# An FNet and SwiGLU mix on one core: x loaded in one piece, a weight's load ahead of two stores, the comparisons of O1 placed anew, and a register load ahead of the last stores

## The chip, the core and the metric

The kernel runs on one core of a Trainium2 chip. The metric is the device time of one execution in microseconds (us), from the program's launch to its end on that core; lower is better. A profile of one execution comes with it. Its span runs from the first to the last instruction, and its times count from the span's start. The engines have short names: PE is TensorE (matrix products), PEld its weight loads, DVE is VectorE, ACT is ScalarE, POOL is GpSimd, and SP is SyncE, which does nothing here but issue transfers (DMAs) and decide the branch at the end.

## The reference

```
x = A_x                                      # 2048 x 512
g = sigmoid((x * gate_w).sum(-1))            # one gate per row
a = dft_hid_re and dft_hid_im applied to x   # along the 512 columns
y = dft_seq_re @ a_re - dft_seq_im @ a_im    # along the 2048 rows
b = (silu(x @ w1) * (x @ w3)) @ w2           # 512 -> 1376 -> 512
out = g * y + (1 - g) * b
```

All in float32. The four DFT matrices are inputs like the others; the kernel may use their structure only if they have it.

## The kernel before

**Numbers in two parts.** TensorE multiplies a shortened float32 format (F32R). Each operand is split into a high part, which ScalarE writes as a copy (`high`, L113), and a low part, the rest, which VectorE makes by a subtraction (`low`, L116). One product of two operands is then three matmuls: high by high, high by low, low by high (`mm3`).

**The SwiGLU branch** comes first, until about 210 us. The products with w1 and w3 run as 22 items, each a chunk of 128 of the 1376 columns by half of the rows; the first is written out by itself, the others are `gate_up(1)` to `gate_up(21)`. A two-by-two block scheme needs seven block products instead of eight for an item; for it VectorE makes sums and differences of x's blocks (tiles `xs_B`, then `xo`) and of w's blocks (`ws`, then the high and low parts `wa` and, from the sums `wu` of `sums_wb`, `wb`). `gate_up(n)` writes out one item by hand: the order of its products, copies and stores is the order of the lines, on every engine. Its `prod(x, n, 4, 4)` is copied by ScalarE into h (L361), the next item's first product waits for a copy out of its PSUM bank, and ScalarE's silu L398 empties the last product. h goes to DRAM by two POOL stores (`store_h`, L320) and its tile has two buffers, so a new h waits until the stores of the one before last have landed. `low_wb` (L244) also stores wb to DRAM by POOL (L248), because the second half of the rows uses it again. The load of a later chunk's w (`load_w`, L198) is POOL's as well; `NEXT_W` says which item issues which load, and at (n, 1) it comes behind `low_wb`.

**The head.** SyncE loads the first quarter of w's first chunk, then x's block B11 in two halves (`load_xo(0, "B11", 2)`, tiles of 256 KB each), then the rest of that w and the other blocks of x. While these come, PE runs eleven warm-up products (L413). The first half of B11 is split by ScalarE and VectorE together and the first products `C` start with it; the next step, `a`, needs the rest of w.

**The stage of w2** (products H, about 210 to 324 us) multiplies h, loaded back, by w2. Beside it the other engines do two things: they prepare forms of x for the Fourier branch, and they compare the given DFT matrices with themselves. A DFT matrix is full of equal and opposite rows. So only one representative piece (`rep`) of each group O1a, O1b, O2 and E2 is multiplied, and for every other piece VectorE subtracts it from, or adds it to, the representative (`differ`, L730 to L736), and ScalarE sums the absolute values (`add_up`, L741).

**The planner.** These comparisons are tasks in a list. The code is run once when the program is built, and every call `work(engine, us)` puts as many ready tasks of that engine at that place in its order as fit the budget `us`. A task costs 1.2 (VectorE) or 1.1 (ScalarE), may pass the budget by 0.3, and is only taken when its load was asked for at least `LAG` calls before (4 in the stage of w2 and in O1). `work_until` issues all that is left.

**The Fourier branch** (from 324 us). For each of two parts p the products of O1 run into PSUM; ScalarE copies one bank to `e` (L1234); VectorE makes its sum and difference with the other bank (L1235, L1236); `high` and `low` make z_O1 of it. Then follow O2 and E2. Ten output units (L1282 on) multiply z by the hidden DFT; VectorE adds each product times the gate to the SwiGLU part, (1 - g) * b (L1303), and SyncE stores the rows (L1305). Units 0 to 5 have two parts of 128 rows, units 6 to 9 one.

**The end.** When all absolute sums are there, `verdict` (L568, L570) reduces them on VectorE behind unit 3. `sum_flags` (L573) adds them over the partitions on PE, ahead of unit 7's products, and `see_flags` (L576) compares the result behind unit 7's sums. Behind the last unit all five engines load that flag into a register (L1318) and branch (L1325): if the matrices aren't DFT matrices, a second, plain computation follows. In the profiled execution the branch is skipped. SyncE then waits for the last stores to land, and the program ends.

Of the kernel before, what the change touches and what calls it, by code (L numbers as in the profile page):

```python
# [9 lines left out]
I32 = mybir.dt.int32  # L10
# [5 lines left out]
D = 512  # L16
# [14 lines left out]
def fnet_swiglu_gate_kernel(  # L31
# [25 lines left out]
    nc = tc.nc  # L57
# [54 lines left out]
    def high(hi, src):  # L112
        nc.scalar.activation(hi, src, AF.Copy)  # L113

    def low(hi, lo, src):
        nc.vector.tensor_sub(lo, src, hi.bitcast(F32))  # L116
# [36 lines left out]
    XO, ST = {}, {}  # L153
    XRAW = ("B12", "B11", "B21", "B22")
# [9 lines left out]
            XO[2] = xo1.tile([P, 2, 2, 512], F32R, tag="xo6", name="xo1_6")  # L164
        return XO[2]

    def load_xo(g, k, pieces=1):

        if g not in XO:
            XO[g] = (xo1 if g else xo0).tile([P, 2, 7 - g, 2, 512], F32R, tag="xo", name=f"xo{g}")  # L170
        ST[g, k] = wide(f"xs{g}_{k}")
        n = 1024 // pieces
        for i in range(pieces):
            nc.sync.dma_start(ST[g, k][:, i * n : i * n + n], xt[g, XRAW.index(k), :, i * n : i * n + n])

    OPS = ("B11", "B21", "B22", "T1", "T2", "T3", "T4")
    SUMS = {"T1": ("B12", "B11"), "T2": ("B22", "T1"), "T3": ("B22", "B12"), "T4": ("B21", "T2")}
# [14 lines left out]
    def back(w):  # L192
        return w >= NC and SETS[w] > 0

    def load_w(w, lo=0, hi=4, by=nc.gpsimd):
        if lo == 0:
            WS[w] = f4_a.tile([P, 4, 256], F32, tag=f"f4_{4 + w % (LOOK + 1)}", name=f"ws{w}")
        by.dma_start(WS[w][:, lo:hi].rearrange("p a n -> p (a n)"), w13[SETS[w], :, lo * 256 : hi * 256])  # L198
# [27 lines left out]
    def sums_wb(w):  # L226

        r = WS.pop(w)
        u = WU[w] = wup.tile([P, 4, 256], F32, tag="wu", name=f"wu{w}")
        nc.vector.tensor_add(u[:, 2], r[:, 3], r[:, 2])  # L230
        nc.vector.tensor_sub(u[:, 0], u[:, 2], r[:, 0])
        nc.vector.tensor_sub(u[:, 1], r[:, 0], r[:, 3])
        nc.vector.tensor_sub(u[:, 3], r[:, 1], u[:, 0])
# [5 lines left out]
    def high_wb(w):  # L239
        for half in range(2):  # L240
            new_wb(w, half)
            high(*wb_parts(w, half)[::2])
# [89 lines left out]
    NEXT_W = {}  # L332
    for w in range(LOOK + 3, len(SETS)):
        v = w - LOOK - 1
        at = (WSET.index(v) - LOOK, 0) if back(v) else (WSET.index(v) - 1, 1)
        NEXT_W.setdefault(at, []).append(w)

    def gate_up(n):
        last = NI - 1
        x, s1 = G.pop(n)  # L340
        z = bank(6 + n % 2, f"Z{n}")
        if n >= NI - 3:
            h = HR[n - NI + 3] = wide(f"h{n}")
        else:
            h = hp.tile([P, 1024], F32, tag="h", name=f"h{n}")
        u2, g1 = h[:, :512], h[:, 512:]
        u4 = u4p.tile([P, 512], F32, tag="u4", name=f"u4_{n}")
        nw = WSET[n + 1] if n < last else 0
        if nw == 0 or nw == WSET[n] or len(WB.get(nw, ())) == 2:
            nw = None  # L350
        elif back(nw):
            load_wb(nw, 1)
            nw = None
        wa = WSET[n + LOOK + 1] if n + LOOK < last else 0
        if wa in WA or wa == 0:
            wa = None
        for w in NEXT_W.get((n, 0), ()):
            load_w(w, 0, 3)

        prod(x, n, 4, 4, False, True)  # L360
        nc.scalar.activation(u2, x, AF.Copy)  # L361
        run(early, n)
        prod(z, n, 5, 5, True, True)
        run(ahead, n)
        nc.scalar.activation(u4, z, AF.Copy)
        run(second, n)
        if nw is not None and n > 1:
            sums_wb(nw)
        if n + LOOK <= last:
            first1(n + LOOK)  # L370
        if nw is not None and n > 1:
            high_wb(nw)
        if n + 2 < NI - 3 and back(WSET[n + 2]):
            load_wb(WSET[n + 2], 0)
        prod(x, n, 3, 3, False, True)
        nc.vector.tensor_add(u4, u4, x)  # L376
        if nw is not None and n == 1:
            sums_wb(nw)
            high_wb(nw)
        if nw is not None:  # L380
            low_wb(nw)
        for w in NEXT_W.get((n, 1), ()):
            load_w(w, 0, 3 if back(w) else 4)
        run(mid, n)
        prod(z, n, 2, 6, False, True)
        nc.vector.tensor_add(u2, u2, z)
        nc.vector.tensor_mul(u2, s1, u2)  # L387
        store_h(n, 0, u2)
        if wa is not None:
            new_wa(wa)  # L390
            parts_a = wa_parts(wa, 0, 3)
            high(parts_a[0], parts_a[2])
        if n + LOOK <= last:
            first2(n + LOOK)
        if wa is not None:
            low(*parts_a)
        prod(x, n, 6, 2, False, True)
        nc.scalar.activation(g1, x, AF.Silu)  # L398
        put_score(n, 1, x)
        if n + LOOK <= last:  # L400
            gate1(n + LOOK)
        nc.vector.tensor_mul(g1, g1, u4)
        store_h(n, 1, g1)
        run(at_end, n)
# [1 line left out]

    ctx.enter_context(tc.manual_schedule())
    load_w(0, 0, 1, nc.sync)
    load_xo(0, "B11", 2)
    warm = nc.const_aps.tensor(1.0, [P, 512], mybir.dt.bfloat16)  # L410
    wps = bank(7, "wps")
    for n in range(WARM):
# [143 lines left out]
    n = NI - 1 - LOOK  # L556
# [5 lines left out]
    flag = tail[:, 144:160]  # L562
# [545 lines left out]
    for m, (half, c) in enumerate(HSTEPS):  # L1108
        i = m % NC
# [11 lines left out]
        h, w = HT[m][1], WT[i]  # L1121
# [91 lines left out]
    def load_nb(u):  # L1213
        n, k = UNITS[u][3], FIRST[u]
        if k < 8:
            NB[u] = NBK[k // 2]
            return
        NB[u] = wide(f"nbr{u}")
        nc.sync.dma_start(NB[u].rearrange("p (k n) -> p k n", k=2)[:, :n],
                          nbsp[k - 8 : k - 8 + n].rearrange("k p n -> p k n"))  # L1220
# [4 lines left out]
    for p in range(2):  # L1225
        t = next_two(f"O1_{p}")
        ps = t[:, :512], t[:, 512:]
        for par in range(2):
            forms(ps[par][:, :256], ps[par][:, 256:], ("O1a", "O1b"), (par,), p)
            if par == 0:  # L1230
                work("A", 1.2 if p else 2.4)
                work("D", 1.3)
        e, s = wide(f"e{p}"), wide(f"s{p}")
        nc.scalar.activation(e[:, :512], ps[0], AF.Copy)  # L1234
        nc.vector.tensor_add(s[:, :512], e[:, :512], ps[1])  # L1235
        nc.vector.tensor_sub(s[:, 512:], e[:, :512], ps[1])  # L1236
        free(e)
        t = parts(f"z_O1{p}").rearrange("p h a n -> p h (a n)")
        high(t[:, 0], s)
        low(t[:, 0], t[:, 1], s)  # L1240
        free(s)
        Z["O1", p] = t
        work("D", 1.2)
    t = parts("z_O2").rearrange("p h a n -> p h (a n)")
    two = next_two("O2")
    for p in range(2):
# [18 lines left out]

    for u in range(6, len(UNITS)):
        load_nb(u)
    z_E = yp.tile([P, 2, 2, 516], F32R, tag="z_E2", name="z_E2")

    def even(p):  # L1270
# [8 lines left out]
    for u, (kind, za, zb, n, swap) in enumerate(UNITS):  # L1279
        if u == 4:  # L1280
            even(1)
        ps = next_two(f"Y{u}")  # L1282
        if u == 7:
            sum_flags(ps)

        def zs(p, at):
            return [Z[kind, p][:, h, at : at + P] for h in range(2)]

        evens = ps[:, 250:510].rearrange("p (b n a) -> p b n a", b=2, a=2)
        odds = ps[:, 512:768].rearrange("p (b n a) -> p b n a", b=2, a=2)  # L1290
        chain_two(evens, [(zs(0, za), same_d(0, 130)), (zs(1, zb), both_d(0, 130))])
        chain_two(odds, [(zs(1, za), same_d(130, 258)), (zs(0, zb), both_d(130, 258))])
        r = yp.tile([P, 1024], F32, tag=f"r{u % 6}", name=f"r{u}")
        nb = NB.pop(u)

        def pair(lo, hi):
            return ps[:, lo : lo + 2 * (hi - lo)].rearrange("p (a m) -> p a m", a=2)[:, :, :P]

        for i in range(n):
            k = FIRST[u] + i  # L1300
            rv, nv = (v[:, i * D : i * D + D].rearrange("p (a h n) -> p a h n", a=2, h=2) for v in (r, nb))
            for h, src in enumerate((pair(380, 640), pair(251, 512)) if i ^ swap else (pair(250, 512), pair(381, 640))):
                nc.vector.scalar_tensor_tensor(rv[:, :, h], src, g_pos[:, k : k + 1], nv[:, :, h],  # L1303
                                               op0=ALU.mult, op1=ALU.add)
        nc.sync.dma_start(out[FIRST[u] : FIRST[u] + n].rearrange("k p n -> p k n"),  # L1305
                          r.rearrange("p (k n) -> p k n", k=2)[:, :n])
        if FIRST[u] > 7:
            free(nb)
        if u < 2:
            work("A", 3.6)  # L1310
            work("D", 1.3)
        if u == 2:
            work_until(set(range(n_late)))
        if u == 3:
            verdict()
        if u == 7:
            see_flags(ps)
    bad = nc.values_load(flag.bitcast(I32)[0:1, 2:3], min_val=0, max_val=0x3F800000,  # L1318
                         skip_runtime_bounds_check_because="a comparison's result, 0.0 or 1.0")
    close(zo_a_cm, lp_cm)  # L1320
    close(mov_cm, sp_cm, hh_cm, f4d_cm, y_cm)

# [242 lines left out]
```

## Time and profile before

| | us |
|---|---|
| median of 3 runs | 362.36 (361.52 to 362.67) |
| the profiled execution | 362.3 |
| its span | 360.5 |
| PE busy in the span | 350.8 (97%) |
| DVE busy | 310.0 (86%) |
| ACT busy | 234.2 (65%) |
| POOL busy | 102.8 (29%) |

The profile is read by its views. The waits say which engine stood idle for whom: total, number of times, longest. A row of the timeline has the start, the length, the engine, the line, the operation, the tiles (out<-in), their shapes and the number of instructions merged in it, and in brackets the idle time just before with what ended it. The starts of neighbouring instructions lie closer than their lengths, since one begins while the one before still writes. The DMA rows have the number of transfers, KB each and the median from issue to landing. A row for a stretch has its length, the busy time of an engine with the number of instructions, the granted clock of TensorE, the DMA engines' share and GB/s.

### The profile page before, as it was taken

How to read it: one execution, taken by the hardware profiler on the slowest of the kernel's cores; microseconds unless marked ns; L12 is line 12 of the kernel's file. 1: busy time of each engine (PE TensorE's matmuls, PEld its weight loads, DVE VectorE, ACT ScalarE, POOL GpSimd, SP SyncE). 2: the span in 40 equal slices, each digit the busy share in tenths (PEclk: the TensorE clock that was granted, in tenths of full speed). 3: DMA queues.
4: the chain of work that ended last, by engine and by line, in shares of the span. 5: the costliest groups of instructions: out<-in, count | busy, mean ns of one | idle time of the engine just before them, and what ended most of it. 6: DMA issues, size and time to landing. Idle time of an engine off the chain costs nothing.

```text
span 360.5 us, 5136 instructions
## 1 busy us (share of the span) xinstructions
PE 350.8 (97%) x1720; PEld 303.6 (84%) x1720; DVE 310.0 (86%) x433; ACT 234.2 (65%) x394; POOL 102.8 (29%) x118
## 2 busy tenths in 40 slices
PE   8999999999999999999999999999999999999992
PEld 3888878888888888888888888888888888889892
DVE  2999889999868888878887799989979699998883
ACT  4776566656649587775433499453778988996750
POOL 0011323233211132111111833425030049994000
PEclk9999999999999999999999999999999999999998
DMA  7738967768836769999999259984489999996165
GB/s 237 286 120 282 371 257 239 249 235 313 300 118 210 223 207 395 399 403 407 358 398 273 85 192 371 409 325 146 145 345 375 413 403 369 414 406 209 52 252 211
DMA packets 33857, 102.78 MB, mean 285 GB/s; under 512 B 5922, under 2 KB 6179, under 8 KB 33828
## 3 DMA queue, kind: packets, MB, share of 16 engines
q1 hardware_dynamic: 26340, 75.67, 57.1%
q0 software_dynamic: 7488, 26.75, 20.9%
q8 instruction: 14, 0.23, 0.3%
q14 instruction: 15, 0.12, 0.1%
HBM read 77.76 MB, written 24.65 MB: 284 GB/s over the span
## 4 chain that ended last, share of the span: by engine, by line


## 5 line engine op out<-in xcount | busy, mean ns | idle before, releaser
L127 PE MATMUL H<-w2t,ht 128*128 128x512 f32 (+1 forms) x528 | 114.4, 379 | 0.1
L127 PEld LDWEIGHTS H<-w2t,ht 128*128 128x128 f32 (+1 forms) x528 | 99.7, 189 | 14.6 <-DVE w2t L116 0.5
L127 PE MATMUL X<-xo,wb 128*128 128x512 f32 x378 | 88.8, 379 | 0.2 <-DMA wb<-wbsp 0.2
L127 PEld LDWEIGHTS X<-xo,wb 128*128 128x128 f32 x378 | 71.2, 189 | 11.1 <-issue 0.6
L741 ACT ACTIVATE t<-t 128x1024 f32<-128x1024 f32 (+1 forms) x68 | 67.7, 997 | 8.8 <-DVE t L730 5.8
L320 POOL DMA_DIRECT2D hs<-h x36 | 19.7, 547 | 86.8 <-DVE h L387 59.1
L765 POOL TENSOR_SCALAR mov_E<-mov_E 128x2 fp32r<-128x2 f32 x2 | 35.4, 17697 | 22.3 <-DVE mov_E L116 22.3
L730 DVE TENSOR_TENSOR t<-t,rep 128x1024 f32<-128x1024 f32 x28 | 33.2, 1217 | 0.0
L127 PE MATMUL X<-xo,wa 128*128 128x512 f32 x126 | 30.9, 381 | 0.3 <-ACT h L398 0.3
L398 ACT ACTIVATE h<-X 128x512 f32<-128x512 f32 x21 | 12.5, 594 | 28.4 <-PE X L127 28.3
L376 DVE TENSOR_TENSOR u<-u,X 128x512 f32<-128x512 f32 x21 | 14.4, 686 | 19.0 <-PE X L127 11.7
L127 PE MATMUL Y<-xo,wa 128*128 128x512 f32 x126 | 30.6, 379 | 0.0
L127 PE MATMUL Z<-xo,wb 128*128 128x512 f32 x126 | 30.6, 379 | 0.0
L127 PE MATMUL Z<-xo,wa 128*128 128x512 f32 x126 | 30.6, 379 | 0.0
L732 DVE TENSOR_TENSOR t<-t,rep 128x1024 f32<-128x1024 f32 x24 | 28.2, 1217 | 0.0
L127 PEld LDWEIGHTS X<-xo,wa 128*128 128x128 f32 x126 | 23.6, 189 | 4.4 <-ACT h L398 0.7
L127 PEld LDWEIGHTS Y<-xo,wa 128*128 128x128 f32 x126 | 23.8, 189 | 3.4
L127 PEld LDWEIGHTS Z<-xo,wb 128*128 128x128 f32 x126 | 23.8, 189 | 3.4
L127 PEld LDWEIGHTS Z<-xo,wa 128*128 128x128 f32 x126 | 23.8, 189 | 3.4
L113 ACT ACTIVATE ht<-hr 128x1024 fp32r<-128x1024 f32 x19 | 19.9, 1049 | 9.7 <-issue 4.8
L248 POOL DMA_DIRECT2D wbsp<-wb x16 | 8.8, 553 | 57.5 <-DVE wb L116 56.7
L116 DVE TENSOR_TENSOR wa<-ws,wa 128x768 fp32r<-128x768 f32 (+1 forms) x22 | 19.3, 879 | 6.2 <-ACT wa L113 6.0
(199 smaller groups left out, 526.0 us busy)
## 6 DMA issues: line engine op xcount, KB each, us to landing
t<-wt SPq DMA_DIRECT2D x60, 512.0 KB, 8.0
hr<-hs SPq DMA_DIRECT2D x19, 512.0 KB, 7.3
hs<-h POOLq DMA_DIRECT2D x36, 256.0 KB, 5.8
wbsp<-wb POOLq DMA_DIRECT2D x16, 512.0 KB, 4.5
wb<-wbsp SPq DMA_DIRECT2D x16, 512.0 KB, 9.0
xr<-xw SPq DMA_DIRECT2D x8, 512.0 KB, 11.8
xs_B<-xt SPq DMA_DIRECT2D x7, 512.0 KB, 6.5
ws<-w POOLq DMA_DIRECT2D x6, 512.0 KB, 6.0
```

The source lines that it names most:

```text
L113: nc.scalar.activation(hi, src, AF.Copy)
L116: nc.vector.tensor_sub(lo, src, hi.bitcast(F32))
L127: nc.tensor.matmul(ps.rearrange("p (n a) -> p n a", a=2), u, turns(v)[:, some], **kw)
L248: nc.gpsimd.dma_start(wbsp[w, half], WB[w][half].bitcast(F32))
L320: nc.gpsimd.dma_start(hs[c][:, b * TB : (b + 1) * TB], h)
L376: nc.vector.tensor_add(u4, u4, x)
L398: nc.scalar.activation(g1, x, AF.Silu)
L730: nc.vector.tensor_sub(t, t, r)
L732: nc.vector.tensor_add(t, t, r)
L741: nc.scalar.activation(t[:, :n], t[:, :n], AF.Abs, accum_out=acc[:, i : i + 1])
L765: nc.gpsimd.tensor_scalar(MV[kind][:, :, par, 128], MV[kind][:, :, par, 0].bitcast(F32), 1.0 - 2.0 * par, None, op0=ALU.mult)
```

## The change

It has four parts. x's first block is loaded by one DMA of 512 KB instead of two of 256 KB. In `gate_up` the load of a later w, `NEXT_W` at (n, 1), is issued right behind `sums_wb`, ahead of the stores in `low_wb` (and ahead of the next first product's lines when n > 1). In O1 the calls of the planner get other places and budgets. The flag is summed and compared at unit 6 instead of 7, SyncE loads it into its register there, so ahead of the stores of units 7 to 9, and the other four engines load it behind the last unit as before.

```diff
-    def load_xo(g, k, pieces=1):
+    def load_xo(g, k):
...
-        n = 1024 // pieces
-        for i in range(pieces):
-            nc.sync.dma_start(ST[g, k][:, i * n : i * n + n], xt[g, XRAW.index(k), :, i * n : i * n + n])
+        nc.sync.dma_start(ST[g, k], xt[g, XRAW.index(k)])
...
+    def next_w(n):
+        for w in NEXT_W.get((n, 1), ()):
+            load_w(w, 0, 3 if back(w) else 4)
...
         if nw is not None and n > 1:
             sums_wb(nw)
+            next_w(n)
         if n + LOOK <= last:
             first1(n + LOOK)
...
         if nw is not None and n == 1:
             sums_wb(nw)
+            next_w(n)
             high_wb(nw)
         if nw is not None:
             low_wb(nw)
-        for w in NEXT_W.get((n, 1), ()):
-            load_w(w, 0, 3 if back(w) else 4)
...
-    load_xo(0, "B11", 2)
+    load_xo(0, "B11")
...
             if par == 0:
                 work("A", 1.2 if p else 2.4)
-                work("D", 1.3)
+                work("D", 0.0 if p else 2.5)
         e, s = wide(f"e{p}"), wide(f"s{p}")
         nc.scalar.activation(e[:, :512], ps[0], AF.Copy)
+        work("A", 1.2)
         nc.vector.tensor_add(s[:, :512], e[:, :512], ps[1])
         nc.vector.tensor_sub(s[:, 512:], e[:, :512], ps[1])
         free(e)
         t = parts(f"z_O1{p}").rearrange("p h a n -> p h (a n)")
         high(t[:, 0], s)
+        work("D", 1.3 if p else 0.0)
         low(t[:, 0], t[:, 1], s)
         free(s)
         Z["O1", p] = t
-        work("D", 1.2)
...
+    bad_in, seen = nc.alloc_registers("bad"), flag.bitcast(I32)[0:1, 2:3]
...
-        if u == 7:
+        if u == 6:
             sum_flags(ps)
...
-        if u == 7:
+        if u == 6:
             see_flags(ps)
-    bad = nc.values_load(flag.bitcast(I32)[0:1, 2:3], min_val=0, max_val=0x3F800000,
-                         skip_runtime_bounds_check_because="a comparison's result, 0.0 or 1.0")
+            nc.sync.reg_load(bad_in[mybir.EngineType.SP], seen)
+    for e in (nc.gpsimd, nc.scalar, nc.tensor, nc.vector):
+        e.reg_load(bad_in[e.engine], seen)
+    bad = nc.snap(bad_in, donate=True, min_val=0, max_val=0x3F800000)
```

## The prediction

> **What bounds the kernel now.** I read the page first, then the cores, then TensorE's waits, and only then the stretches that the edits touch.
>
> ```profile
> core 0: 360.5 us, clock 0.996
> ```
> ```profile
> PE 350.8 (97%) x1720; PEld 303.6 (84%) x1720; DVE 310.0 (86%) x433; ACT 234.2 (65%) x394; POOL 102.8 (29%) x118
> ```
> ```profile
> PE Y L1263 <- DVE z_O L116: 0.8, 1, 0.8
> PE X L127 <- ACT h L398: 0.3, 1, 0.3
> ```
>
> TensorE (PE) is busy 350.8 of 360.5 us at a granted clock of 0.996. From 30 us on its two longest waits sum to 1.1 us. So there are three places to win: the head, where PE waits for data; the few waits in between; and the tail, from the last transforms to the end of the program. The tail is not PE's:
>
> ```profile
> 331.54 2.35 DVE L736 TENSOR_TENSOR t<-t,rep 128x1024 f32<-128x1024 f32 x2
> 333.81 0.68 DVE L1235 TENSOR_TENSOR s<-e,O 128x512 f32<-128x512 f32 x1
> 334.41 0.68 DVE L1236 TENSOR_TENSOR s<-e,O 128x512 f32<-128x512 f32 x1
> 336.22 1.23 DVE L116 TENSOR_TENSOR z_O<-s,z_O 128x1024 fp32r<-128x1024 f32 x1 [1.13 <-ACT z_O L113]
> 337.36 1.22 DVE L116 TENSOR_TENSOR z_O<-O,z_O 128x1024 fp32r<-128x1024 f32 x1
> 338.49 0.42 DVE L116 TENSOR_TENSOR z_E<-E,z_E 128x258 fp32r<-128x258 f32 x1
> 339.36 0.43 DVE L116 TENSOR_TENSOR z_E<-E,z_E 128x258 fp32r<-128x258 f32 x1 [0.45 <-ACT z_E L113]
> 339.70 6.35 DVE L1303 SCALAR_TENSOR_TENSOR r<-Y,tail,nb 128x256 f32<-128x256 f32 x16
> 346.65 0.24 DVE L568 SCALAR_TENSOR_TENSOR tail<-tail 128x80 f32<-128x80 f32 x1 [0.59 <-ACT t L741]
> ```
> ```profile
> 353.06 1.68 DVE L1303 SCALAR_TENSOR_TENSOR r<-Y,tail,nbr 128x256 f32<-128x256 f32 x4
> ```
>
> This is VectorE's timeline. From 331.54 to its last output sum, which ends at 353.06 + 1.68 = 354.74, it stands idle for only 1.13, 0.45 and 0.59 us in these rows. It carries the tail, so what shortens VectorE's order there brings the last store forward. The work between the quoted stretches is left as it is.
>
> **Comparisons between the parts of O1.** Two comparisons (331.54, 2.27 us up to the next start, so 1.135 each) stand ahead of the second part's add (L1235). The add needs only ScalarE's copy e:
>
> ```profile
> 331.31 0.58 ACT L1234 ACTIVATE e<-O 128x512 f32<-128x512 f32 x1
> 335.12 1.06 ACT L113 ACTIVATE z_O<-s 128x1024 fp32r<-128x1024 f32 x1 [3.23 <-DVE s L1236]
> ```
>
> The copy is there at 331.89; the add starts at 333.81. To see where the comparisons go I followed the rule of `work` by hand: one is taken only if its budget covers its cost (1.2, less 0.3) and if four planner calls have passed since its load was asked for. Three are left when O1 begins. Their loads were asked for in the two VectorE calls of the last chunk of half 0 and in O1's first ScalarE call, so at O1's first VectorE call they are 4, 3 and 1 calls old. The budget of 2.5 therefore still takes one. The second goes between the high and low of the second part, where the new budget of 1.3 stands; the third goes to the unchanged call behind O2's split.
>
> So the add comes at about 331.9, 1.9 earlier. ScalarE's high part follows at 335.12 - 1.9 = 333.2; the sum of absolute values put ahead of it, about 1.04, begins at 331.85 and ends at 332.9, in a wait that was 3.23. The comparison between high and low lies beside ScalarE's high part: it takes 1.135 where VectorE stood idle 1.13, and costs nothing. If that cover were gone it would cost its 1.135. The low part then starts at 336.22 - 1.87 = 334.35 and ends at 335.6, and O2's low part moves as far. The third comparison adds 1.135 before the E parts: 338.49 becomes about 337.75. From there the order is the same, so the first sixteen output sums start 0.74 earlier.
>
> Behind them VectorE waited 0.59 for ScalarE's last absolute sums:
>
> ```profile
> 339.20:346.52 7.32, 7.29 (x14) 1.00 0.53 197
> ```
>
> This is ScalarE, the absolute sums alone: fourteen instructions, seven sums with their read-outs, 1.04 each, until 346.52. The new order runs two of the seven before the E parts, and the others start 0.7 earlier, so they end near 346.5 - 2 x 1.04 - 0.7 = 343.7; the verdict is due at 339.70 - 0.74 + 6.35 = 345.3. The wait is gone with 1.6 to spare. Together 0.74 + 0.59 = 1.33.
>
> PE must follow. It waited inside the first output unit for the low part, and it takes the flag's product in the unit starting here:
>
> ```profile
> 337.50 0.71 PE L1263 MATMUL Y<-dt,z_O 128*128 128x260 f32 x4 [0.77 <-DVE z_O L116]
> ```
> ```profile
> 347.76 1.71 PE L1263 MATMUL Y<-dt,z_E 128*128 128x260 f32 x12
> ```
>
> With the low part there at 335.6 the product at 337.50 can come at 337.50 - 0.77 - 0.4 = 336.3 (0.4: the slow products around the stall, an estimate from 0.71 for four). PE gains about 1.2, and VectorE's end is held to that within 0.1. I take **1.3**, with bounds of 0.7 (the sums still come last) and 1.4. The flag's product, moved from unit 7 to unit 6, now waits for the verdict with 48 output products behind it on PE. The verdict ends some 0.5 after 345.3 and PE is there at 347.76 - 1.2 = 346.5: 0.7 of cover; each us beyond it would be one us of PE.
>
> **SyncE's register load.**
>
> ```profile
> L1318 SPq TENSOR_LOAD <-tail x1: 752/752/752, 355.1 to 355.1; - x1
> ```
> ```profile
> 353.94 1.16 SPq L1305 DMA_DIRECT2D out<-r  x2
> ```
> ```profile
> SPq L1325 <- SPq L1325: 2.3, 2, 1.9
> ```
> ```profile
> out<-r SPq DMA_DIRECT2D x1, 256.0 KB, 4.1
> ```
> ```profile
> out<-r SPq DMA_DIRECT2D x1, 256.0 KB, 2.7
> ```
> ```profile
> q8 instruction: 1, 0.02, 1.2%
> q14 instruction: 3, 0.02, 1.0%
> ```
>
> The load takes 0.752 us behind the last store's issue, but afterwards SyncE waits 1.9 for that store to land (4.1 us from its issue). Taking the load out of that place is worth **nothing** by itself. At its new place it waits for the flag's comparison on VectorE, and the stores of units 7, 8 and 9 are queued behind it. Units come 1.68 / 2 = 0.84 apart. The last store's issue runs from 354.74, when its sum is done, to 355.10: about 0.35. So the load delays unit 7's store by 0.35 + 0.75 + 0.05 - 0.84 = 0.3; unit 8 is nearly on time, unit 9 fully. That holds until the load takes about 0.75 + 2 x 0.84 - 2 x 0.35 - 0.3 = 1.4; beyond, each us is one us at the end.
>
> What can move is the landing. The store before it landed in 2.7, so the last one lost 1.4. In the window from 354.7 to 361 one packet of the instruction queue q8 held a DMA engine for 1.2% of 16 x 6.3 = 1.2 us. These are code fetches behind the branch, and one engine delivers its share of the store behind them. The flag is now known one unit (0.84) sooner, so the loads and branches of ScalarE, GpSimd and SyncE come 0.7 to 0.8 earlier against the last store; PE's is held by its own products. Bounds: -1.4 (clear of the fetch, the 2.7 row) and +0.3 (one third of q14's 1.0 us more in the way). I take **-0.3**, near the 4.1 row, as PE's large fetch keeps its place. The Trainium skill (Runtime: NRT & Kernel Launch, Instruction fetch mechanics) says that a taken branch to code outside the fetched window must first fetch it. The trace agrees (four instruction packets in the tail), and as the branch stays, by that rule alone the tail gains 0 and the sum below would be 0.3 less.
>
> **x in one piece.**
>
> ```profile
> 1.28 0.90 SPq L174 DMA_DIRECT2D xs_B<-xt  x2
> ```
> ```profile
> 5.69 0.42 ACT L113 ACTIVATE xo<-xs_B 128x256 fp32r<-128x256 f32 x1 [2.06 <-DMA xs_B<-xt]
> 6.37 0.63 ACT L113 ACTIVATE xo<-xs_B 128x512 fp32r<-128x512 f32 x1 [0.26 <-DMA xs_B<-xt]
> 7.93 0.42 ACT L113 ACTIVATE a<-ws 128x256 fp32r<-128x256 f32 x1 [0.94 <-DMA ws<-w]
> ```
> ```profile
> 6.16 0.70 PE L127 MATMUL C<-xo,wa 128*128 128x512 f32 x2 [0.38 <-ACT xo L113]
> 7.05 1.21 PE L127 MATMUL C<-xo,wa 128*128 128x512 f32 x4 [0.19 <-ACT xo L113]
> 8.40 0.94 PE L127 MATMUL C<-xo,a 128*128 128x512 f32 x3
> ```
>
> One issue of 0.45 goes, and the loads behind it on SyncE's queue are issued that much sooner. The first half no longer arrives ahead (5.69). But PE's next step, at 8.40, waits for w's rest (7.93), not for x. If all of x is there at time T, ScalarE needs 0.42 + 0.6 for x and 0.42 for a, so PE goes on at T + 1.5: anything up to T = 6.9 is hidden, and both halves are there at 6.37 now. What counts is how far w's rest moves: between 0 (the transfers' rate sets it) and 0.45 (the issue sets it). I take **-0.25**, the middle, with a bound of +0.9 if x lands late (last rival). From 8.40 PE runs on almost without a gap, so the shift reaches the end. The Trainium skill (Perfetto Trace Analysis, DMA Optimizations) speaks against this edit: smaller DMAs may start sooner. The trace agrees for the first half (5.69 against 6.37), not for the step that sets PE; by that rule alone the head gains nothing and the sum is 0.25 less.
>
> **w's load ahead of wb's stores.**
>
> ```profile
> 34.55 1.14 POOL L248 DMA_DIRECT2D wbsp<-wb  x2 [8.97 <-DVE wb L116]
> 35.68 0.54 POOL L198 DMA_DIRECT2D ws<-w  x1
> ```
> ```profile
> ACT wa L113 <- DMA ws<-w: 2.9, 1, 2.9
> ACT h L361 <- DMA hs<-h: 0.6, 1, 0.6
> ```
> ```profile
> 46.91 1.64 PE L127 MATMUL X<-xo,wa 128*128 128x512 f32 x6 [0.31 <-ACT h L398]
> 48.59 0.70 PE L127 MATMUL X<-xo,wb 128*128 128x512 f32 x2
> ```
>
> ScalarE waits 2.9 for this load, and with it L398, PE's 0.31 at 46.91. Ahead of the two stores the load lands sooner and that stall goes. But the next step, at 48.59, needs ScalarE's L361, which waits for a store of h to free its tile. That store stands on POOL's queue behind the load and both wb stores, in whichever order: the bytes ahead of it are the same. PE arrives earlier and waits longer. I take **0**, with bounds of -0.6 (h's store also comes sooner) and +0.2.
>
> **The sum.** 1.3 + 0.3 + 0.25 + 0 = 1.85, call it 1.9. The profiled execution took 362.3 (span 360.5 and 1.8 around it); the median of the runs is 362.36, the same within 0.1. Forecast: 360.4.
>
> **Rivals.**
>
> *The last landing clears the code fetch*: 2.7 instead of 4.1, 1.1 more than I take: 359.3. For it: four engines branch earlier. Against: PE's fetch hangs on its last products. 0.14.
>
> *h's store isn't the next stall*: w's load brings 0.6: 359.8. Against: the 0.6 wait on that very store. 0.10.
>
> *The absolute sums stay last, or the planner packs the comparisons otherwise*: only 0.7 of 1.3 comes: 361.0; with no gain at the landing 361.3. For: two engines' orders must both fit. 0.16.
>
> *x in one piece lands late*, the slower side. The place is the first step, the price one us per us beyond T = 6.9. It decides against the change from T = 6.9 + 1.65 = 8.55.
>
> ```profile
> xs_B<-xt SPq DMA_DIRECT2D x7, 512.0 KB, 6.5
> ```
>
> The other x pieces, of 512 KB, took 6.5 from issue to landing (they queue behind each other): T = 7.8, and the time is 361.5, about no change. Landing 9 after its issue, near 10.3, it would make 364. For: those rows. Against: nothing but 128 KB of w is queued ahead of it. 0.07 for the first, 0.04 for the second.
>
> The forecast keeps 0.49; its own range is 359.9 to 361.0.
>
> **How the numbers follow.** About 0.3% (1.1 us, so 361.3) is what a measurement of this kernel can tell from no change. Faster: the forecast, the first two rivals and nearly a third of the third, 0.49 + 0.14 + 0.10 + 0.04 = 0.77, less 0.01 for cases not thought of. Same: the rest of the third and the first late landing, 0.19. Slower: 0.05. The range reaches from the cleared landing to the late x: 359.2 to 361.6.
>
> **What would show it.** Right: the add L1235 of the second part within 0.1 behind its copy e, with no comparison ahead of it; PE's 0.8 wait on z_O gone; L568 without a wait; VectorE's last sum 1.5 earlier; SyncE's register load between the stores of units 6 and 7. PE's 0.31 at 46.91 gone and a longer gap at 48.59. Wrong: VectorE idle before L568, the last store's landing beyond 4.4, the step at 8.40 later than now, or the whole span shorter by under 1.

## The result, and the profile after

The changed kernel takes 359.29 us (median of 7 runs, 358.31 to 359.86); the kernel before, run beside it, 361.52 (7 runs, 360.89 to 362.67). The ratio is 0.9932, 95% interval 0.9913 to 0.995, so 1.8 to 3.1 us. A second set gave 359.16 (5 runs) against 361.05 (21 runs), 0.9954 (0.994 to 0.9967), so 1.2 to 2.2 us. Faster, by about 2 us. The forecast of 360.4 is missed by 1.1, while its step of 1.9 lies in both intervals.

The execution profiled took 358.31, the fastest of its seven, with a span of 356.5; the one of before, 362.3, was among the slowest of its kernel. The two traces therefore differ by 4.0, where the medians differ by 2.2. Which part of this belongs to the edits is what the experiments are for.

The core, and the busy times of the page:

```profile
core 0: 356.5 us, clock 0.994
```
```profile
PE 348.1 (98%) x1720; PEld 303.7 (85%) x1720; DVE 309.7 (87%) x433; ACT 234.3 (66%) x394; POOL 102.6 (29%) x118
```

The clock is within 0.002 of the one before, and TensorE's busy share has risen to 98%. Of the 4.0, 1.3 is idle time of TensorE (9.7 before, 8.4 now). The other 2.7 is busy time of the same 1720 matmuls: those near a wait are drawn out, as the six at 46.91 in the profile before, which took 1.64, where the same six take 1.46 here. TensorE's waits, all that the view lists: total, times, longest.

```profile
PE wps L415 <- PEq L1558: 0.9, 1, 0.9
PE C L127 <- ACT xo L113: 0.6, 1, 0.6
```

The waits of 0.8 on z_O and 0.3 behind L398 are gone; what is left is in the first 6 us. VectorE's timeline from the second part of O1 on:

```profile
329.25 0.69 DVE L1238 TENSOR_TENSOR s<-e,O 128x512 f32<-128x512 f32 x1 [0.30 <-ACT e L1236]
329.86 0.68 DVE L1239 TENSOR_TENSOR s<-e,O 128x512 f32<-128x512 f32 x1
330.46 1.22 DVE L738 TENSOR_TENSOR t<-t,rep 128x1024 f32<-128x1024 f32 x1
331.67 1.23 DVE L116 TENSOR_TENSOR z_O<-s,z_O 128x1024 fp32r<-128x1024 f32 x1
332.81 1.22 DVE L116 TENSOR_TENSOR z_O<-O,z_O 128x1024 fp32r<-128x1024 f32 x1
333.94 1.22 DVE L738 TENSOR_TENSOR t<-t,rep 128x1024 f32<-128x1024 f32 x1
...
336.29 6.35 DVE L1307 SCALAR_TENSOR_TENSOR r<-Y,tail,nb 128x256 f32<-128x256 f32 x16
342.56 0.23 DVE L570 SCALAR_TENSOR_TENSOR tail<-tail 128x80 f32<-128x80 f32 x1
...
348.11 0.13 DVE L578 TENSOR_SCALAR tail<-Y 1x1 f32<-1x1 f32 x1
348.17 2.42 DVE L1307 SCALAR_TENSOR_TENSOR r<-Y,tail,nbr 128x256 f32<-128x256 f32 x6
```

The second part's add stands right behind its copy e, with no comparison ahead. One comparison fills what was VectorE's idle 1.13 between high and low (330.46), the third follows O2's low part (333.94), and the verdict L570 comes without a wait. From the add to the start of the first output sums it is 336.29 - 329.25 = 7.04; before, from the copy's end at 331.89, it was 7.81.

The tail, by the DMA view from just ahead of the last store, and SyncE's register load:

```profile
q8 instruction: 1, 0.02, 0.6%
...
out<-r SPq DMA_DIRECT2D x1, 256.0 KB, 4.1
```
```profile
L1322 SPq TENSOR_LOAD <-tail x1: 876/876/876, 348.6 to 348.6; - x1
```

The load moved as it should. The last store still lands 4.1 after its issue, with one 16 KB code packet (q8) beside it. The q8 packets go with TensorE's instructions and are taken for its code: the profile of before has 14 of them, one for every 202 to 280 of its matmuls and weight loads.

### The profile page after: what moved, and what is told of

It is laid out like the page before. It is cut to its first block, busy times and chain, and to the rows that moved or that the text cites. A ratio compares the mean times of both kernels' runs of the same rounds, so it can differ in the third digit from the quotient of the medians.

```text
span 356.5 us, 5140 instructions
## 1 busy us (share of the span) xinstructions
PE 348.1 (98%) x1720; PEld 303.7 (85%) x1720; DVE 309.7 (87%) x433; ACT 234.3 (66%) x394; POOL 102.6 (29%) x118
## 4 chain that ended last, share of the span: by engine, by line
PE 72%; DVE 16%; DMA 6%; issue 3%; ACT 1%; SPq 0%; DVEq 0%
PE X L127 31%; PE H L127 15%; PE Z L127 15%; PE Y L127 8%; DVE t L732 4%; DVE r L1307 3%; PE C L127 3%; DMA t<-wt 3%; DVE t L734 2%; DVE ht L116 2%; DMA rep<-wt 2%; DVE t L738 2%; DMA xs_B<-xt 1%; DVE z_O L116 1%; DVE s L1238 0%
## 5 line engine op out<-in xcount | busy, mean ns | idle before, releaser
L116 DVE TENSOR_TENSOR ht<-hr,ht 128x1024 fp32r<-128x1024 f32 x19 | 23.1, 1218 | 0.0
```

## The experiments

The kernels of the experiments were run in four sets; those of a set share one chip and its runs of the kernel before. The two kernels of the result were run in a set of their own. "Faster" below is the kernel before less the kernel, from the ratio. One reading serves many of them: the starts of TensorE's 1720 matmuls, counted in order of time. "61st" is the start of the 61st, behind the head; "61 to 301" the time from it to the 301st, about 70 us, in which the two waits at 46.9 and 48.6 fall; "1301 to last" is the end of the w2 stage with O1 and the output; "tail" runs from the last matmul's start to the end of the span.

| kernel | us, median | ratio to before | 61st | 61 to 301 | 1301 to last | tail |
|---|---|---|---|---|---|---|
| before (profile shown) | | | 18.04 | 52.89 | 66.01 | 6.98 |
| before, second profile | 361.68 (one run) | | 17.45 | 51.93 | 66.02 | 7.06 |
| x in one piece alone | 360.62 | 0.9991 (0.9975 to 1.0007) | 16.59 | 52.17 | 66.33 | 7.09 |
| w's load ahead alone | 361.68 | 1.0008 (0.9992 to 1.0024) | 18.26 | 51.93 | 66.31 | 7.18 |
| O1 alone | 359.87 | 0.9958 (0.9939 to 0.9976) | 17.33 | 53.17 | 64.55 | 6.88 |
| flag alone | 361.57 | 0.9997 (0.9979 to 1.0015) | 17.46 | 52.01 | 65.79 | 7.41 |
| changed, profile shown | 359.29 | 0.9932 (0.9913 to 0.995) | 16.52 | 51.92 | 64.47 | 7.18 |
| changed, again | 359.16 | 0.9954 (0.994 to 0.9967) | 16.75 | 51.93 | 64.46 | 7.62 |
| changed without x | 360.03 | 0.9967 (0.9951 to 0.9983) | 17.22 | 51.93 | 64.58 | 7.43 |
| changed without w | 359.82 | 0.9972 (0.9958 to 0.9986) | 17.61 | 51.93 | 64.58 | 7.51 |
| changed without O1 | 360.76 | 0.9991 (0.9976 to 1.0006) | 16.48 | 51.93 | 65.82 | 7.60 |
| changed without flag | 359.58 | 0.9963 (0.995 to 0.9976) | 16.99 | 51.92 | 64.57 | 7.32 |
| x in four pieces | 362.77 | 1.0043 (1.0023 to 1.0064) | 18.88 | 52.59 | 66.00 | 7.32 |
| x in one piece and a dummy load | 361.45 (one run) | | 17.41 | 52.23 | 66.35 | 7.16 |
| register load late | 358.91 | 0.9939 (0.9917 to 0.9961) | 16.54 | 52.98 | 64.47 | 6.99 |
| no branch | 356.47 | 0.987 (0.9851 to 0.9889) | 16.47 | 51.92 | 64.47 | 5.05 |
| small body | 357.37 | 0.9908 (0.9876 to 0.994) | 16.48 | 51.93 | 64.47 | 6.29 |
| both gaps filled | 358.19 | 0.9919 (0.9902 to 0.9937) | 16.95 | 51.92 | 64.47 | 6.35 |

The kernel before had medians of 361.07 (35 runs), 360.97 (23), 361.10 (12) and 361.05 (21) in the four sets, and 361.52 (7) beside the result. The two kernels with one run have no ratio; only their traces count.

**Each part alone**, in the kernel before. Each edit is that part of the change's diff; only its main lines are shown here and below, and "..." stands for the rest.

```diff
...
-    load_xo(0, "B11", 2)
+    load_xo(0, "B11")
```

> x in one piece alone. By the prediction's theory (only w's rest sets the step of product a, and the transfers' rate holds it) this is 0.25 us faster than before and product a comes at about 8.15 us. By the rival theory, read from the trace after (a at 7.24 against 8.40), the one large transfer moves the whole stream of first loads: product a comes before 7.6 and the time falls by 1.0 to 1.5. A third reading: the two traces differ by chance in the head, then the time is within 0.3 of before while a single trace may show anything from 7.2 to 8.4.

```diff
...
             sums_wb(nw)
+            next_w(n)
...
```

> w's load ahead of wb's stores alone. By the prediction's theory the stall of 0.3 before the product at 46.9 goes, but the next one at 48.6 grows by as much, because the bytes ahead of h's store are the same: time within 0.2 of before. By the rival theory, from the trace after, both stalls go: 1.0 faster, and h's store lands over 1 us sooner against the products than in the trace before.

```diff
-                work("D", 1.3)
+                work("D", 0.0 if p else 2.5)
...
+        work("A", 1.2)
...
+        work("D", 1.3 if p else 0.0)
...
-        work("D", 1.2)
```

> The comparisons of O1 alone. By the prediction's theory 1.3 faster (bounds 0.7 and 1.4), the second part's add right behind its copy e, no wait ahead of the verdict. By a rival in which something else than VectorE's order holds the end (the last stores' landing), under 0.5.

```diff
...
-        if u == 7:
+        if u == 6:
             see_flags(ps)
+            nc.sync.reg_load(bad_in[mybir.EngineType.SP], seen)
...
```

> The flag at unit 6 and SyncE's early register load alone. By the prediction's theory 0.3 faster, bounds 1.4 faster and 0.3 slower. By the rival, from the trace after (the last store still lands 4.1 us after its issue), nothing: within 0.2. By a third theory it costs: in this kernel the comparisons still come late, PE meets the flag's product in unit 6 before the verdict is there, and the three stores behind the register load are pressed together: 0.2 to 0.6 slower.

O1 alone is 0.9 to 2.2 faster and is the only part whose interval lies clear of no change (a ratio of 1). The four sum to 1.7 (0.32 - 0.29 + 1.52 + 0.11). With x alone `a` came at 7.17, as the rival had it, but the time did not fall by its 1.0. With w's load alone the stretch from the 61st to the 301st matmul was free of waits, as the rival had it, and the time did not fall at all.

**The whole without one part.** Four kernels undo one part of the changed kernel, by the edits above turned around; the last is the changed kernel once more.

> The change without its part in O1: x, w's load and the flag together. If the parts add as they measured alone (x 0.3 faster, w 0.3 slower, flag 0.1 faster, each within 0.6) this is 0 to 0.5 faster than before. If they work only together (a shorter head moves the stalls of the SwiGLU stage, which w's early load then removes), it is 1.0 or more faster, as the whole measured 2.4 where the four alone sum to 1.7.

> The changed kernel with x's first block in two pieces again. In five traces with two pieces the 61st matmul of PE starts at 17.3 to 18.3, in seven with one piece and nothing added at 16.5 to 17.0. Theory A (that 1.0 reaches the end): 61st matmul at 17.3 to 18.3, and 0.9 to 1.0 slower than the changed kernel run beside it. Theory B (most of it is given back on the way, as 0.3 for the part alone suggests): 61st matmul as late, but 0.2 to 0.4 slower.

> The changed kernel with w's load behind wb's stores again. From the 61st to the 301st matmul PE takes 51.92 us where it never waits; over that it took 0.97, 0.01, 1.25, 0.09, 0.67, 0.25, 0.31 in seven traces with the load behind, and 0.01, 0, 1.06, 0, 0, 0, 0 in seven with the load ahead. Theory A (the load ahead makes these waits rarer): some of them here, and 0.2 to 0.5 slower than the changed kernel. Theory B (they come by chance in both): the same time within 0.2.

> The changed kernel with the flag at unit 7 and all five register loads behind the last store again. Theory A (this part brings nothing, its landing stays at about 4.1): within 0.3 of the changed kernel. Theory B (it brings the 0.3 forecast, or more): 0.3 to 1.4 slower, with the last store landing later than 4.1 or the end more than 5.9 behind the last output sum.

> The changed kernel once more, as the measure for the three beside it. Theory A (the terms read from the traces, x 1.0, w 0.35, O1 1.5, all reach the end): 2.5 to 2.9 below the kernel before, ratio 0.992 to 0.993. Theory B (the timed single parts: x 0.3, w -0.3 to 0.2, O1 1.5): 1.7 to 1.9 below, ratio about 0.995.

The changed kernel once more is 1.7 below the kernel before, as theory B has it. Without O1 the gain is 0.3 of the 1.7 to 2.45, and both signs of the old order are back. Its TensorE and VectorE timelines:

```profile
335.47 5.08 PE L1265 MATMUL Y<-dt,z_O 128*128 128x260 f32 x43 [0.77 <-DVE z_O L116]
```
```profile
344.61 0.24 DVE L570 SCALAR_TENSOR_TENSOR tail<-tail 128x80 f32<-128x80 f32 x1 [0.58 <-ACT t L743]
```

By the medians beside the changed kernel's 359.16, leaving out x costs 0.87, w 0.66, the flag 0.42; by the ratios 0.5, 0.65, 0.3. Each is uncertain by about 0.7, so none of the three is shown by itself. For x the middle lies between theory A's 0.9 and B's 0.3.

**The head.** Is it the number of pieces, the issue that is saved, or chance? Three kernels: x in four pieces; x in one piece with a load of 64 bytes that nothing uses right behind it; the kernel before again.

```diff
-    load_xo(0, "B11", 2)
+    load_xo(0, "B11", 4)
```

> The kernel before with x's first block in four pieces of 128 KB instead of two of 256 KB. If the number of issues ahead of w's rest sets the head, each costs about 0.47: product a some 0.9 later than with two pieces and the time 0.5 to 0.9 longer. If only the size of the packets counts, also longer, 0.2 to 0.5. By the splitting rule of the Trainium skill (Perfetto Trace Analysis, DMA Optimizations) smaller pieces start sooner: the first product comes before 4.7 and the time is the same or shorter.

```diff
...
-    load_xo(0, "B11", 2)
+    load_xo(0, "B11")
+    nc.sync.dma_start(tail[:1, 100:116], edges[:, :16])
```

> The kernel before with x's block in one piece, and behind it on SyncE's queue one load of 64 bytes that nothing uses, so that the loads behind are issued as late as with two pieces. Theory A (the steady early start of one piece comes from the issue that is saved): a at about 7.65 and the first products with B21 at about 9.65, 0.45 later than the 7.2 and 9.2 of the kernels with one piece. Theory B (it comes from how the transfers of one piece run, not from the issue): a at 7.2 to 7.3 and B21 at 9.1 to 9.3 as in those.

> The kernel before once more, unchanged, for a second profile. Theory A (the first arrivals of x in two pieces, and the two waits at 46.9 and 48.6, are chance from execution to execution): the step a starts anywhere from 7.0 to 8.6 (8.40 in the profile shown, 6.99, 7.44 and 8.59 in kernels whose head is the same), and the waits of 0.31 and more at 46.9 and 48.6 need not both come again; the profiled time is then 360.3 to 361.5. Theory B (they belong to the kernel): a at 8.3 to 8.6, both waits there, and a profiled time near 362.3.

TensorE's timeline of the head: the products `a`, then those with block B21. The changed kernel:

```profile
7.24 1.46 PE L127 MATMUL C<-xo,a 128*128 128x512 f32 x6
8.54 2.75 PE L127 MATMUL C<-xo,wa 128*128 128x512 f32 x12
```

The kernel before, second profile:

```profile
7.81 1.59 PE L127 MATMUL C<-xo,a 128*128 128x512 f32 x6 [0.29 <-ACT a L113]
9.24 2.98 PE L127 MATMUL C<-xo,wa 128*128 128x512 f32 x12
```

One piece and the dummy load:

```profile
7.17 1.46 PE L127 MATMUL C<-xo,a 128*128 128x512 f32 x6
9.03 3.15 PE L127 MATMUL C<-xo,wa 128*128 128x512 f32 x12 [0.40 <-ACT xo L113]
```

Four pieces:

```profile
8.52 1.46 PE L127 MATMUL C<-xo,a 128*128 128x512 f32 x6
10.50 2.72 PE L127 MATMUL C<-xo,wa 128*128 128x512 f32 x10 [0.52 <-ACT xo L113]
```

Chance first: the same kernel before shows `a` at 8.40 in one execution and 7.81 in the next, and the 61st matmul at 18.04 and 17.45. Over all traces the 61st comes at 17.22 to 18.26 with two pieces (six traces, median 17.45) and at 16.47 to 17.61 with one (ten, median 16.57): 0.9 earlier in the middle, with overlap. Four pieces give 18.88, and they did not bring the first product ahead of 4.7: it came at 5.35.

The 0.9 has two parts. The step `a` itself starts at 7.25 in the middle with one piece and at 7.70 with two, 0.45 sooner, which is one issue. From `a` to the 61st matmul PE then needs 9.28 to 9.42 in all ten traces with one piece and 9.64 to 10.34 in all six with two: with two the products behind `a` wait, or are drawn out. The dummy load separates them: `a` starts as early as with one piece (theory B), yet PE waits 0.40 ahead of the next products, and the 61st matmul comes at 17.41. That is what two pieces give in the middle, but it is a single trace, and one kernel with one piece and nothing added came at 17.61. So it is not shown that 64 bytes ahead cost as much as 256 KB, and why the second part comes stays open.

The waits near 47 and 48.6 vary from execution to execution too. The second profile of the kernel before has neither (51.93 from 61st to 301st, where the shown profile took 0.96 more). Over eight traces with w's load behind the stores that stretch is 0.0 to 1.25 longer than 51.92, 0.45 on average; over ten with the load ahead it is free of it in nine. More than 0.2 was lost in five of the eight and in one of the ten; whether the load ahead makes the waits rarer, or the executions fell that way, is not settled by so few. The tenth, the kernel with the late register load, shows what the wait is when it comes:

```profile
44.94 1.46 PE L127 MATMUL X<-xo,wa 128*128 128x512 f32 x6
47.18 1.56 PE L127 MATMUL X<-xo,wb 128*128 128x512 f32 x6 [0.78 <-ACT h L363]
```

It is the step on h (L363, before L361). A further stretch, from the 601st to the 901st matmul, takes 64.75 to 65.79 in the eighteen traces, on average the same with the load ahead (65.09) as behind (65.13): what one profile shows there says nothing about the edits.

**The tail.** What holds the last store? No branch: the second computation, its branch and the register loads are left out, the flag is still computed. Late load: SyncE's register load goes back behind the last store. Small body: of the second computation one load of x is left.

```diff
...
-    for e in (nc.gpsimd, nc.scalar, nc.tensor, nc.vector):
-        e.reg_load(bad_in[e.engine], seen)
-    bad = nc.snap(bad_in, donate=True, min_val=0, max_val=0x3F800000)
...
```

> The changed kernel with the second computation, the branch and the register loads left out; the flag is still computed, and nothing is done with it. If the code fetches behind the branch hold the last store's landing, it lands in 2.7 to 2.9 us instead of 4.1 and the kernel is 1.2 us faster than the changed kernel, some 3.6 faster than before. If the landing is held by the stores themselves, which come back to back at the end, it still takes 4.1 and the time is that of the changed kernel within 0.4.

```diff
-            nc.sync.reg_load(bad_in[mybir.EngineType.SP], seen)
-    for e in (nc.gpsimd, nc.scalar, nc.tensor, nc.vector):
+    for e in (nc.sync, nc.gpsimd, nc.scalar, nc.tensor, nc.vector):
```

> The changed kernel with SyncE's register load back behind the last store, the flag still at unit 6. By the prediction's theory the load at its new place delays unit 7's store by 0.3 and not the last, and at the old place it is hidden behind the landing: same as the changed kernel within 0.3. By a rival in which the three stores pressed together land later because of the load, the landing falls from 4.1 and this is 0.3 or more faster than the changed kernel.

```diff
-        xa = [get(gen, f"x{q}", 1024) for q in range(8)]
...
-                nc.sync.dma_start(out[k], y)
+        xa = get(gen, "x0", 1024)
+        nc.sync.dma_start(xa, xs[0])
```

> The changed kernel with the code behind the branch cut down: the second computation is left out but for one load of x, so the branch and the five register loads stay and the code that a core would have to fetch past the branch is small. Kernels with the full body land their last store 3.9 to 4.45 us after its issue and end 5.7 to 6.3 us behind the last output sum; without any branch it was 2.8 and 3.8. Theory A (the fetches of the code behind the branch hold the last store): with few or no instruction packets in the tail the landing falls to about 2.8, the end comes about 4.6 behind the last sum, and the time is 1.0 to 1.4 below the changed kernel's, near 357.6 (ratio to the kernel before near 0.990). Theory B (the register loads and the branch themselves hold the end): landing and end stay, time near 358.8 (ratio near 0.994).

The DMA view from the last store on. No branch (there is no row of a q8 packet):

```profile
q1 hardware_dynamic: 411, 0.74, 17.7%
issues: line engine op xcount, KB each, median us to landing
out<-r SPq DMA_DIRECT2D x1, 256.0 KB, 2.8
```

Late load:

```profile
q8 instruction: 1, 0.02, 0.7%
...
out<-r SPq DMA_DIRECT2D x1, 256.0 KB, 3.9
```

Small body:

```profile
q8 instruction: 1, 0.02, 0.5%
...
out<-r SPq DMA_DIRECT2D x1, 256.0 KB, 4.0
```

Without the branch the packet is gone and the store lands in 2.8, 1.3 sooner. The small body did not do what it was built for: its packet stays, and so does the landing. It does end sooner, and SyncE's waits say where. Changed kernel, then small body:

```profile
SPq L1331 <- SPq L1331: 3.4, 4, 1.8
```
```profile
SPq L1529 <- DMA out<-r: 2.7, 3, 1.8
```

In the changed kernel SyncE's waits for the stores stand at the branch (L1331), and from the landing to the end of the span another 1.8 go by: 356.5 less the landing at 350.6 + 4.1. Twelve semaphore steps of SyncE, 0.7 together, stand behind that landing. In the small body the waits stand at the program's last line, those steps run while the stores land, and 1.0 goes by. So the landing that theory A expected did not come, and a time near its own (357.37 for 357.6) came for another reason; the time's interval overlaps the changed kernel's and reaches B's 0.994. From the last output sum to the end, no branch and the full body differ by both, about 2.1. The late load loses nothing that these runs can tell.

**Both gaps filled.** One more planner call puts a comparison into VectorE's idle time in O1's first part as well, so none is left behind O2's split.

```diff
-        work("D", 1.3 if p else 0.0)
+        work("D", 1.3)
```

> The changed kernel with one more planner call of 1.3 between VectorE's high and low step of O1's first part, so that one comparison lies there in VectorE's idle time (1.13 in the profile before) too and none is left behind O2's split. Theory A (VectorE still carries the stretch from O1 to the end after the change): the first output sums start about 1.1 earlier, and so does the end: near 357.8, ratio to the kernel before near 0.991. Theory B (after the change PE carries it: its last product ends at about the time at which the last output sums start): the first sums start earlier but the last ones do not; 0 to 0.2 us faster than the changed kernel, ratio near 0.994.

VectorE's timeline at its end:

```profile
348.65 0.88 DVE L1307 SCALAR_TENSOR_TENSOR r<-Y,tail,nbr 128x256 f32<-128x256 f32 x2 [0.42 <-PE Y L1266]
349.99 0.88 DVE L1307 SCALAR_TENSOR_TENSOR r<-Y,tail,nbr 128x256 f32<-128x256 f32 x2 [0.47 <-PE Y L1266]
```

VectorE now waits for PE, and PE's 1301 to last is 64.47, as in the changed kernel: theory B, the change has made the end PE's. The time is 0.5 to 1.3 below the changed kernel's by the ratios, more than theory B's 0.2, and PE gave nothing of it. The trace shows a tail of 6.35 for 7.18: VectorE is now late behind PE, so the code packet comes 0.73 ahead of the end of the last sum instead of 0.37 behind it, and the last store lands in 3.3. It is the best kernel here that does all the work, though its interval overlaps the changed kernel's.

## Why the prediction was right and wrong

**The step that failed** is the base, the number from which the sum is taken: "The profiled execution took 362.3 (span 360.5 and 1.8 around it); the median of the runs is 362.36, the same within 0.1. Forecast: 360.4." The two agreed, but both were high. The kernel before stands at 361.0 to 361.1 in four sets of 12 to 35 runs. The profiled execution had a head 0.6 later than the next profile of the same kernel (18.04 against 17.45) and the waits at 47, which that one lacks: 0.96. Three runs with 1.15 us between them couldn't tell. Of the 1.1 by which 360.4 was missed, 0.84 is the base (361.52 beside the result for 362.36) and 0.27 the terms. From the 361.1 of the larger sets, the same 1.9 gives 359.2, and 359.29 and 359.16 were measured.

**The comparisons of O1: right.** The order came out as worked out by hand, call by call. Copy to first sums fell by 7.81 - 7.04 = 0.77 (forecast 0.74), the verdict's wait of 0.59 went, PE's 1301 to last fell from 66.0 to 64.5 (eight traces without the part 65.8 to 66.35, ten with it 64.46 to 64.58). The time is 1.5 (0.9 to 2.2) for the forecast's 1.3. That the flag's product would not wait at unit 6 held as well. "It carries the tail" is true of VectorE before, no more after: the last filling showed PE's 64.47 as the floor.

**SyncE's register load: the landing did not come sooner.** "I take **-0.3**." The load delayed unit 7's store (it starts 0.97 ahead of the last sum's end, before 1.63: 0.66 for the 0.3 worked out) and took 0.876 and not 0.752. In six traces with the early load the last store lands in 4.1 to 4.55, in eight with all loads late 4.0 to 4.3, in the kernel with only SyncE's load late 3.9. So the sign "beyond 4.4" appeared in the second profile of the changed kernel (4.55) and in the one without O1 (4.45).

The traces show where it went. "PE's large fetch keeps its place" is what failed: the 16 KB packet came earlier, 0.37 behind the last sum in the changed kernel instead of 1.49. It had held up only the last store, and now it holds up the last two. A landing is recorded in sixteen parts. In the profile of before, 13 parts of the last store are there after 2.27 and the last after 4.06; the store of unit 8 lands whole in 2.74, ahead of the packet's end. In the changed kernel unit 8's store has 15 parts there after 2.95 and the last after 4.04 as well. With all loads late the last store lands 1.41 to 1.48 behind the packet's end (eight traces); with the early load 2.66 to 2.73 (these six and the kernel with both gaps filled). That the late parts queue behind the packet on one DMA engine fits these numbers, though no view names the engine. In four of the six, SyncE's issue itself was held, until 0.34 to 0.37 behind the packet's end. In the second profile of the changed kernel:

```profile
351.23 2.20 SPq L1309 DMA_DIRECT2D out<-r  x1
```

With all loads late the last issue took 0.33 in every trace. By the sentence on the Trainium skill (Runtime: NRT & Kernel Launch, Instruction fetch mechanics) the tail was to gain 0; the traces, 0.2 later on average, are nearer to that than to the 0.3. The timed difference, 0.1 to 0.4 faster with the part, doesn't settle a few tenths.

**x in one piece: right in sign, mis-sized.** "What counts is how far w's rest moves: between 0 ... and 0.45." Traces show 0.9 at the 61st matmul. The step `a` did move by the upper bound, 0.45 in the middle. What was put at nothing is the block behind it ("From 8.40 PE runs on almost without a gap"): with two pieces PE needs at least 0.36 more there, up to 1.06. The late x did not come: it landed at 5.0 to 5.6 in nine traces of the ten, at 6.2 in the other. About 0.2 is given back near 110 us: the stretch from the 301st to the 601st matmul is 64.97 to 64.98 in all eleven traces with one piece and 64.75 in all seven with more; two matmuls at 109.8 take 0.1 more each, a cause I did not find. The time is 0.3 alone, 0.5 to 0.9 in the whole, each uncertain by 0.7: 0.7 by the traces fits both. The rule of the Trainium skill (Perfetto Trace Analysis, DMA Optimizations) that smaller DMAs may start sooner is borne out by the first piece's landing alone. It came at 3.93 with four pieces, at 4.25 to 5.67 with two and at 5.03 to 6.19 with one, and yet four pieces made the kernel 0.8 to 2.3 slower.

**w's load: the bound held, the reason not.** "PE arrives earlier and waits longer" at 48.59: in nine of ten traces neither wait is there. But the waits come and go in the kernel before too. The traces' averages differ by 0.3; the times say -0.3 alone and 0.65 in the whole, each uncertain by about 0.7, so a gain of 0 to 0.3 is an estimate and not shown. The changed kernel without this part had no such wait in its one trace and was slower all the same.

Of the rivals none came in: the landing was not cleared, the absolute sums were not last, x was not late, and w's load gave no clear 0.6. "VectorE's last sum 1.5 earlier" was 354.74 - 350.59 = 4.15 in the two profiles shown, as the slow head and the waits of the one before come on top.

The sum of the terms from the traces, with -0.2 for the store that lands later (4.3 on average with the early load, 4.1 without), is 1.55 + 0.7 + 0.3 - 0.2 = 2.35, against 2.45 and 1.7 measured: it lies inside the first interval (1.8 to 3.1) and 0.15 above the second (1.2 to 2.2). The forecast's 1.9 was right partly by luck, because its terms erred both ways: x and O1 gave more by the traces, the register load nothing.

## What to carry to other kernels

Take the base from as many runs as the question needs: a change of 0.5% can't be forecast to a number from three runs whose spread is 0.3%, and the one profiled execution may hold waits that the next doesn't. Before pricing a wait of a few tenths, ask whether it is one of an engine's order (it comes in every trace, as the 0.77 on z_O) or of a transfer's arrival (it comes and goes, as those near 47). When an engine's order at the end has been tightened, look which engine is last then: a further filling of VectorE's gaps found PE.

## What was not expected of the hardware

- With x's first block in two transfers of 256 KB instead of one of 512 KB, TensorE's 61st matmul came 0.9 us later in the middle of the traces; one issue is 0.45. A kernel with 64 bytes added came as late, in a single trace.
- The branch to a second computation that never runs costs 2.4 us, with its register loads: 356.47 against 358.91 for the late load on the same chip. Of it 1.3 is the landing of the last store beside one 16 KB code packet, and some 0.8 is SyncE's chain behind it.
- A code packet can hold the store's issue as well as its landing. In five traces with the early load SyncE's last issue took 0.99 to 2.20 instead of 0.33, and ended 0.34 to 0.37 behind the packet's end each time.
- A code packet that starts ahead of the last store's issue costs less: 3.3 us to the landing instead of 4.1.
